# Dummy matmuls at the start, a searched order of steps and loads, and a last tile in two halves: one change to an attention and MoE kernel

## The chip, the cores and the metric

The kernel runs on one core of one Trainium2 chip. The metric is device time in microseconds (us). Each kernel was run several times, and each run tells its time, its span on the core and the mean clock that TensorE was granted. A run that is more than 1.5% above the fastest of the same kernel is called slow.

Names used below: PE is TensorE (PEld its weight loads), DVE is VectorE, ACT is ScalarE, POOL is GpSimd, SP is the queue of SyncE, which issues DMAs here. L917 is line 917 of a kernel's file, so the same statement has another number in each kernel.

## The reference, cut to what matters

```python
def _attn_ref(q, k, v):                       # 8 batches, 8 heads, 576 tokens, 64 wide
    scores = np.matmul(q, k.transpose(0, 1, 3, 2)) / np.sqrt(D)
    mask_plain = (rel >= 0) & (rel < 32)                               # heads 0-3
    mask_dil = (rel >= 0) & (rel < 128) & (rel % 4 == 0)               # heads 4-7
    ...                                       # mask, softmax
    return np.matmul(attn, v)

def _moe_ref(x, w_in, w_out):                 # x: 4608 x 512, w_in: 512 x 2048, w_out: 2048 x 512
    h = x @ w_in
    g = h * (1.0 / (1.0 + np.exp(-h)))
    return g @ w_out
```

Attention over narrow windows makes x. Two dense layers follow, and they are nearly all of the arithmetic.

## The kernel before

The kernel is written as many small steps. Kinds: `S` scores, `P` and `D` the products with v for the plain and the dilated heads, `XP` and `XD` transposes of x, `TD`, `TA`, `TB`, `TR`, `TS` transposes of q and k, `N` and `V` copies, and the steps of layer 1 (`h`, 16 blocks of w_in for each group of tokens) and layer 2 (`y`, four matmuls each). When the program is built, a small plan decides the order in which the steps are written down and, for some copies, whether DVE or ACT makes them. It keeps its own clock, on which each step and each load has an assumed cost. PE, DVE, ACT and the DMA queues get their work in the written order, and the program chooses nothing at run time.

```python
ORDER = "k0 w0a v0 r0 w1 w0b w2 w3 d1 p1 r1 o0 o1 o2 o3 v1".split()       # loads: w = w_in, o = w_out, rest q, k, v
LOAD_US = {"w": 2.57, "o": 2.57, "d": 3.2, "p": 3.4, "r": 1.7, "v": 2.5, ...}   # assumed costs
...
for t in vraws[::-1]:
    nc.vector.memset(t, 0.0)
...
    # batches 3-7: how the last steps of a batch stand in its list
    order = [("S", 0), ("S", 1), ("P", 0), ..., ("D", 1, 0), ("D", 1, 1), ("D", 1, 2), ("D", 1, 3)]
...
    # a score step, with the cost the plan assumes: 0.32 us, 0.64 us for batch 0
    st = Step(lambda ring, a=a: scores(ring, *a), 0.32 + 0.32 * (b in BIASED), ...)
...
    # x of batches 3-7 goes to DRAM and comes back transposed
    nc.sync.dma_start(out=rows, in_=oD[:, ab]...)
    yield "DMA", 3.0                          # assumed time of the store
    stored(b)
...
def group_gen(g):
    nc.sync.dma_start_transpose(out=x_of(g)[:, :, GT - n :], in_=x_s[t0 : t0 + n])
    yield "DMA", 6.0                          # assumed time of the transposed read
...
def l2(ring, tb, f4):                         # layer 2, one of four parts of an output tile
    ...
    yield "ACT", 0.50
    ob = o32.tile([P, DM], F32, tag="ob", bufs=2, name=f"ob_{g}_{tb}")
    nc.scalar.activation(ob, y, AF.Copy, scale=0.5)
    nc.scalar.dma_start(out=out[t0 + tb * P : t0 + (tb + 1) * P], in_=ob)
...
while att or l1 or l2:                        # the plan: which step is written next
    cands = [(att, it, 1.0) for it in att[:LOOK] if it[0] <= max(1, g1 - 1) + 2]
    ...
    if l1 and g1 <= g2 + 1:
        main.append((l1, l1[0], 1.3))
    cands = main + cands if side > 0.5 else cands + main
```

The softmax here doesn't subtract the row's maximum and nothing guards it: scores larger than these inputs give would overflow.

## Time and profile before

| | before |
|---|---|
| time | 316.49 us, median of three (315.64 to 317.62) |
| span of the profiled run | 314.6 us |
| PE busy | 298.2 us, 95% |
| first matmul | 5.17 us |
| first layer-1 matmul | 18.12 us, then a wait for w_in until 22.41 us |
| last matmul ends | 310.69 us |

The page of the kernel before, parts 1, 2 and 4. Part 1 has busy time, share of the span and number of instructions; part 2 has busy tenths in 40 slices of 7.9 us, with PEclk as the granted clock in tenths; part 4 is the chain of work that ended last:

```profile
PE 298.2 (95%) x2378; PEld 153.8 (49%) x2378; DVE 198.9 (63%) x498; ACT 164.9 (52%) x316; POOL 54.4 (17%) x86
PE   2979899999999999999999999999999999999995
PEclk9999999999999999999999999999999999999999
...
PE 72%; DMA 13%; DVE 7%; POOL 3%; ACT 2%; issue 1%; ACTq 0%; POOLq 0%
```

PE is the bound.

Timeline of PE, kernel before (start, duration, engine, line, operation, count, idle time before it and what ended it):

```profile
7.36 0.68 PE L614 MATMUL s<-mask_d,ident_w 128*128 128x288 f16 x2
...
16.67 0.41 PE L614 MATMUL s<-mask_d,ident_w 128*128 128x288 f16 x2
...
20.17 0.28 PE L671 MATMUL av_d<-vd,probs 128*128 128x65 f16 x4
22.41 0.61 PE L884 MATMUL h<-xA,w_in 128*128 128x256 f16 x4 [1.96 <-DMA w_in<-in_moe_w_in_dram]
...
38.69 1.02 PE L917 MATMUL y<-w_out,gT 128*128 128x512 f16 x4
```

The first two lines are the same pair of matmuls, and the later one takes 0.41 us where the earlier takes 0.68 us; the second matmul starts 0.13 us after the first there, and 0.23 us here. So PE starts at about half its later pace. PEclk does not show this, because the trace's clock records begin only at 14.57 us, with full clock; for the time before, without a record, the page prints full clock too. The next two lines show PE waiting 2 us for weights.

Two timelines of the kernel before, of the SP queue and of PE, at the point where x of a group comes back from DRAM and layer 1 uses it:

```profile
201.54 2.02 SPq L445 DMA_TRANSPOSE xR<-x_s  x1
...
210.47 1.02 PE L884 MATMUL h<-xR,w_in 128*128 128x512 f16 x4
```

The trace's semaphore records put the landing of that transfer at 206.16 us, so x lies ready 4.3 us before its first use.

The end, ACT's timeline of the kernel before:

```profile
310.73 0.60 ACT L928 ACTIVATE ob<-y 128x512 f32<-128x512 f32 x1 [2.85 <-PE y L917]
311.35 0.34 ACTq L929 DMA_DIRECT2D out_dram<-ob  x1
```

### The profile page before, as it was taken

To read this page: it belongs to the slowest core of one execution; us is meant where nothing else is said; L and a number is where in the kernel's file an instruction comes from. 1 tells how busy PE (TensorE), PEld (TensorE's weight loads), DVE (VectorE), ACT (ScalarE), POOL (GpSimd) and SP (SyncE) were. 2 spreads that over 40 slices of the span, in tenths; PEclk is the share of its full clock that TensorE was granted. 3 is DMA by queue.
4 is the path that set the end of the run, shared out by engine and by line. 5 is a ranking of instruction groups with operands and counts; after the bars stand their busy time and mean duration, and the time that the engine had idled before them with its cause. 6 is when DMAs were issued, how large, how long until landed. Compare 5 with 4: busy or idle time off the path is not lost.

```text
span 314.6 us, 6109 instructions
## 1 busy us (share of the span) xinstructions
PE 298.2 (95%) x2378; PEld 153.8 (49%) x2378; DVE 198.9 (63%) x498; ACT 164.9 (52%) x316; POOL 54.4 (17%) x86
## 2 busy tenths in 40 slices
PE   2979899999999999999999999999999999999995
PEld 1658665554545444444454445444444444444441
DVE  6479987799798677855687578548860552355000
ACT  7567774776656465445564544557443453355111
POOL 8854723001800040005000310000000000000000
PEclk9999999999999999999999999999999999999999
DMA  8999999997999969998998899941165001100221
GB/s 107 178 203 191 172 191 205 204 193 134 159 193 196 208 111 208 185 227 151 197 198 196 136 202 195 233 125 52 52 87 169 0 35 43 57 33 2 90 76 67
DMA packets 107092, 44.53 MB, mean 142 GB/s; under 512 B 73272, under 2 KB 102456, under 8 KB 107064
## 3 DMA queue, kind: packets, MB, share of 16 engines
q0 software_dynamic: 48528, 19.86, 51.9%
q1 hardware_dynamic: 53352, 14.85, 27.8%
q10 hardware_dynamic: 5184, 9.44, 8.6%
q8 instruction: 18, 0.29, 0.4%
q14 instruction: 10, 0.08, 0.1%
HBM read 39.81 MB, written 18.28 MB: 185 GB/s over the span
## 4 chain that ended last, share of the span: by engine, by line
PE 72%; DMA 13%; DVE 7%; POOL 3%; ACT 2%; issue 1%; ACTq 0%; POOLq 0%
PE y L917 35%; PE h L884 32%; DMA vp<-in_v_dram 5%; DMA w_in<-in_moe_w_in_dram 3%; DMA nat<-kq_s 3%; DVE gT L895 2%; DMA nat<-in_k_dram 2%; PE s L626 2%; PE av_d L671 2%; PE av_p L671 1%; DVE probs L644 1%; DVE oP L675 1%; POOL w_out L232 1%; DVE oD L675 1%; POOL vp L182 1%
## 5 line engine op out<-in xcount | busy, mean ns | idle before, releaser
L917 PE MATMUL y<-w_out,gT 128*128 128x512 f16 x576 | 138.1, 379 | 0.9 <-ACT ob L928 0.8
L895 DVE SCALAR_TENSOR_TENSOR gT<-th,h 128x512 f16<-128x512 f32 (+1 forms) x160 | 99.0, 629 | 56.8 <-ACT th L893 56.6
L893 ACT ACTIVATE th<-h 128x512 f32<-128x512 f32 (+1 forms) x160 | 88.9, 557 | 83.3 <-PE h L884 67.8
L884 PEld LDWEIGHTS <-w_in 128*128 128x128 f16 x640 | 59.0, 97 | 58.7 <-issue 4.7
L917 PEld LDWEIGHTS <-gT 128*128 128x128 f16 x576 | 53.9, 98 | 60.8 <-issue 1.1
L884 PE MATMUL h<-xR,w_in 128*128 128x512 f16 x320 | 77.4, 379 | 0.1
L884 PE MATMUL h<-xA,w_in 128*128 128x512 f16 (+1 forms) x320 | 63.2, 336 | 4.2 <-DMA w_in<-in_moe_w_in_dram 2.0
L928 ACT ACTIVATE ob<-y 128x512 f32<-128x512 f32 x36 | 21.5, 597 | 40.8 <-PE y L917 40.7
L635 ACT ACTIVATE probs<-s 128x768 f16<-128x768 f32 (+2 forms) x31 | 24.2, 780 | 12.3 <-PE s L626 11.9
L671 PEld LDWEIGHTS <-probs 128*128 128x128 f16 x448 | 21.7, 98 | 13.7 <-DVE probs L644 1.8
L675 DVE TENSOR_TENSOR oD<-av_d,rcps 72x256 f16<-72x256 f32 x64 | 26.9, 421 | 2.2
L675 DVE TENSOR_TENSOR oP<-av_p,rcps 96x256 f16<-96x256 f32 x48 | 20.2, 421 | 1.6
L639 ACT ACTIVATE probs<-s 128x288 f16<-128x288 f32 (+2 forms) x40 | 17.9, 472 | 1.5 <-ACT ob L928 0.9
L644 DVE TENSOR_TENSOR probs<-probs,mask_p 128x768 f16<-128x768 f16 x21 | 11.6, 554 | 10.7 <-ACT probs L635 10.3
L422 POOL COPY fence<-kqT 128x1 f16<-128x1 f16 x10 | 1.8, 190 | 93.3 <-DMA kqT<-kq_s 93.3
L671 PE MATMUL av_d<-vd,probs 128*128 128x65 f16 x256 | 14.0, 196 | 0.2 <-DVE vd L506 0.2
L644 DVE TENSOR_TENSOR probs<-probs,mask_d 128x576 f16<-128x576 f16 (+1 forms) x23 | 11.9, 518 | 3.4 <-ACT probs L639 1.6
L674 DVE RECIPROCAL rcps<-av_d 72x4 f32<-72x4 f32 x64 | 11.0, 172 | 2.7 <-PE av_d L671 2.5
L671 PE MATMUL av_p<-vp,probs 128*128 128x65 f16 x192 | 11.4, 193 | 0.7 <-DVE probs L644 0.6
L165 POOL DMA_DIRECT2D vraw<-in_v_dram x16 | 10.8, 677 | 6.2 <-DVE rcps L674 2.5
L674 DVE RECIPROCAL rcps<-av_p 96x4 f32<-96x4 f32 x48 | 8.2, 171 | 4.6 <-PE av_p L671 4.6
L178 POOL DMA_DIRECT2D vp<-in_v_dram x7 | 10.3, 1467 | 2.9 <-PE s L626 1.8
(89 smaller groups left out, 145.5 us busy)
## 6 DMA issues: line engine op xcount, KB each, us to landing
out_dram<-ob ACTq DMA_DIRECT2D x36, 256.0 KB, 2.1
kq_s<-in_k_dram POOLq DMA_DIRECT2D x5, 576.0 KB, 10.3
kq_s<-in_q_dram POOLq DMA_DIRECT2D x5, 576.0 KB, 12.9
vp<-in_v_dram POOLq DMA_DIRECT2D x7, 384.0 KB, 7.9
w_out<-in_moe_w_out_dram POOLq DMA_DIRECT2D x4, 512.0 KB, 11.0
vraw<-in_v_dram POOLq DMA_DIRECT2D x8, 224.0 KB, 5.3
w_in<-in_moe_w_in_dram POOLq DMA_DIRECT2D x3, 512.0 KB, 11.0
x_s<-oP SPq DMA_DIRECT2D x10, 144.0 KB, 1.9
```

Of the source, the lines that this page charges most:

```text
L165: nc.gpsimd.dma_start(out=vraw[p0 : p0 + m1 - m0, ab].rearrange("p h r d -> p h (r d)"), in_=src[m0:m1],)
L635: nc.scalar.activation(p2, both[:, :, :n], AF.Exp, scale=scale)
L639: nc.scalar.activation(p2[:, i], sp[i][:, :n], AF.Exp, scale=scale)
L644: nc.vector.tensor_tensor(p2, p2, mk, ALU.mult)
L671: nc.tensor.matmul(a[:, i, : D + 1], lhs(i), rhs(i), start=True, stop=True)
L674: nc.vector.reciprocal(rcp[:n], a[:n, :, D : D + 1])
L675: nc.vector.tensor_tensor(o, a[:n, :, :D], rcp[:n, :, None].broadcast_to([n, HN, D]), ALU.mult)
L884: nc.tensor.matmul(h[:, :w], w_in16[:, c, f * P : (f + 1) * P], x_g[:, c], start=(c == 0), stop=(c == HP - 1),)
L893: nc.scalar.activation(th[:, :w], h[:, :w], AF.Tanh, scale=0.5)
L895: nc.vector.scalar_tensor_tensor(gTs[g][:, f, :w], th[:, :w], 1.0, h[:, :w], ALU.add, ALU.mult)
L917: nc.tensor.matmul(y, gTs[g][:, f, tb * P : (tb + 1) * P], w_out16[:, f], start=(f == 0), stop=(f == NFF - 1),)
L928: nc.scalar.activation(ob, y, AF.Copy, scale=0.5)
```

## The change

The intent: raise PE's clock in time that is idle anyhow, fill the holes between matmuls with an order that an offline search found, and shorten the end.

```diff
-    ORDER = "k0 w0a v0 r0 w1 w0b w2 w3 d1 p1 r1 o0 o1 o2 o3 v1".split()
-    LOAD_US = {"w": 2.57, "o": 2.57, "d": 3.2, "p": 3.4, "r": 1.7, "v": 2.5, ...}
+    ORDER = "k0 r0 w0b v0 w0a w1 w2 w3 d1 p1 o0 r1 o1 o2 o3 v1".split()
+    LOAD_US = {"w": 2.57, "o": 2.57, "d": 3.2, "p": 3.0, "r": 2.3, "v": 2.57, ...}
...
-    for t in vraws[::-1]:
-        nc.vector.memset(t, 0.0)
+    warm = vraws[1].rearrange("p a h r d -> p (a h r d)")
+    nc.vector.memset(warm[:, :GT], 0.0)
+    y_warm = ps_y.tile([P, GT], F32, tag="y", name="y_warm")
+    for n in range(8):
+        nc.tensor.matmul(y_warm, warm[:, :P], warm[:, :GT], start=True, stop=True)
+    nc.vector.memset(warm[:, GT:], 0.0)
+    nc.vector.memset(vraws[0], 0.0)
...    (the three step lists in another order; of batches 3-7:)
-                ("S", 0), ("S", 1), ("P", 0), ("P", 1), ("V", 0), ("S", 2), ("S", 3), ("P", 2),
-                ... ("D", 0, 1), ("D", 0, 2), ("D", 0, 3), ("D", 1, 0), ("D", 1, 1), ("D", 1, 2),
-                ("D", 1, 3),
+                ("S", 2), ("S", 0), ("P", 1), ("S", 3), ("S", 4), ("S", 1), ("S", 5), ("P", 0),
+                ... ("D", 1, 1), ("D", 1, 3), ("D", 0, 1), ("D", 0, 2), ("D", 1, 2), ("D", 1, 0),
+                ("D", 0, 0),
...    (x is stored when a counter says that its parts are done, since their order is now free)
...    (the costs that the plan assumes:)
-                    lambda ring, a=a: scores(ring, *a), 0.32 + 0.32 * (b in BIASED), ...
+                    lambda ring, a=a: scores(ring, *a), 0.17 + 0.32 * (b in BIASED), ...
-                lambda ring, f=f: l1(ring, f), 0.01 + w / 595, ...
+                lambda ring, f=f: l1(ring, f), w / 593, ...
...    (layer 2: 0.8633 for 0.87; the last output tile in two halves, the second half's copy:)
+            half = (c1 - c0) // 2
+            nc.scalar.activation(ob[:, :half], y[:, :half], AF.Copy, scale=0.5)
+            nc.scalar.dma_start(out=rows[:, c0 : c0 + half], in_=ob[:, :half])
+            nc.vector.tensor_scalar(ob[:, half:], y[:, half:], 0.5, None, ALU.mult)
+            nc.sync.dma_start(out=rows[:, c0 + half : c1], in_=ob[:, half:])
...    (the limits by which the plan picks)
-        cands = [(att, it, 1.0) for it in att[:LOOK] ...]
+        cands = [(att, it, LIM_PAIR if it[1].mate else LIM_ATT) for it in att[:LOOK] ...]   # 0.4, 1.1
-            main.append((l1, l1[0], 1.3))
+            main.append((l1, l1[0], LIM_L1))                                             # 1.8
-        cands = main + cands if side > 0.5 else cands + main
+        cands = main + cands if side > SIDE else cands + main                            # 0.9
+        if pick is None and g2 < SPARE and l2[0][1].rings and ...:                       # SPARE = 6
+            l2[0][1].rings = ["y", "x", "z"]
```

So there are six parts: dummies, loads, lists, costs, limits and tail. The costs are four numbers (a score step, a layer-1 step, a layer-2 step, the copy of an output tile).

## The prediction

> **What bounds the kernel now.** TensorE. The summary has PE busy 298.2 of 314.6 us (95%), the chain of waits is 72% PE, and from 234 us on it is nothing but layer-1 and layer-2 matmuls back to back (four 512-column matmuls in 0.86 us) until 310.7 us. The two layers alone come to about 248 us at that pace; attention's small matmuls add some 30 us (estimate, from start-to-start times in the timeline). So roughly 36 us is start, tail and holes; only that can be won: 5.2 us before the first matmul; about 6 us of holes and slow matmuls up to 30 us; about 9 us in 30-80 us; about 9 us in 80-240 us (much of it attached to the score matmuls, "issue" before their weight loads, which the change does not remove); 4 us tail.
>
> **Step by step.**
>
> 1. *Dummy matmuls.* [...] a pair of 288-column bias matmuls takes 0.68 us at 7.4 us and 0.41 us at 16.7 us, although the windows view prints a granted clock of 1.00 there. Eight cold 512-column matmuls are about 3.4 us, in idle time, so free. They could shorten batch 0's attention by 2 to 3 us. But group 0's layer 1 needs all of w_in, whose last block stays at its place (it lands near 27.5 us, estimated from the releases of the queue's waits). Its four feature blocks then need 1.7 us, so group 0 ends at 29.3 us at best; now near 29.8. Gain 0.5 us, up to 2 if attention runs ahead better.
>
> 2. *Load order.* w0b now lands before w1, so the 2.0 us wait of PE for w_in (at 20.4-22.4 us) shrinks or moves to 22-27 us: the same bytes must come first. o0 before r1 lets the first layer-2 step start some 2 us before its present 38.7 us; PE waits 0.9 us for DVE near there.
>
> 3. *New order and thresholds.* 32-44 us is DVE-bound (3.8 of 4 us busy per window), 44-49 us waits for vp (lands 49.2 us), 60-76 us is DVE-bound again. Batch 1's dilated averages now come before its plain ones, so DVE works while vp is awaited; SPARE lets layer 2 take the x and z buffers when nothing else is ready. I expect 3 us of the 9 in 30-80 us, 1.5 us of the 9 in 80-240 us.
>
> 4. *Last tile in halves.* After the last matmul now: 0.60 us copy on ACT, then the DMA. Two quarter copies on ACT and DVE at once, smaller DMAs: 0.3 to 0.5 us.
>
> **Sum.** 0.7 + 3 + 1.5 + 0.4, about 5.5 us: 311.0 us, range 307.5 to 314.5. Nearly all of it is on the critical path, since PE is; off it is most of the warm-up.
>
> **What would show it.** 288-column bias matmuls 0.12 us apart before 10 us; first layer-1 matmul near 19.8 us instead of 18.1, and a new wait for w_in after it; group 0's layer 1 still ending at 29-30 us; first layer 2 near 36-37 us; PE denser in 44-52 us; final stretch of pure matmuls unchanged but earlier; last copy under 0.3 us.
>
> **What would make it wrong.** Warm-up too short, or followed by too long a gap, to raise the clock; warm attention running far ahead and gaining over 2 us; transfers landing later than the order assumes, so that PE, strictly in order, stands behind a missing operand; thresholds that fill the later holes much better (below 308).

The 2 to 3 us for batch 0's attention are an estimate of mine. The sum 0.7 + 3 + 1.5 + 0.4 is 5.6 us, written as about 5.5. What step 1 calls eight cold matmuls took 3.59 us in the trace of the changed kernel, starting up to 0.43 us apart, where matmuls of 512 columns start 0.22 us apart later on. Of the two risks named for the clock, that trace shows the second: full clock ended at 8.99 us, in a wait of PE of 1.97 us. That a warm-up can be too short was a guess of mine.

## The result, and the profile after

The changed kernel took 312.63 us in the median of six runs (311.31 to 316.78), against 316.68 us for the kernel before. The ratio of the fast runs is 0.9853 (95% interval 0.9816 to 0.989). A ratio here is the mean time of one kernel's fast runs over that of the other's fast runs of the same rounds, so it is not quite the ratio of the quoted medians. The time lies within the predicted range, 1.6 us above the point.

The median hides something: two of the six runs were slow, at 316.1 and 316.8 us. All twelve runs of the changed kernel (six more came with the experiments) with their mean granted clock:

| mode | us (mean clock) |
|---|---|
| seven runs, mean 312.1 us | 311.31 (1.0), 311.61 (0.988), 311.64 (1.0), 312.10 (1.0), 312.39 (1.0), 312.66 (0.999), 312.88 (1.0) |
| five runs, mean 316.3 us | 315.31 (0.982), 316.02 (0.994), 316.11 (0.984), 316.78 (0.984), 317.38 (0.984) |

The split at 315 us is mine. By the 1.5% rule three of the five longer runs are slow; 315.31 and 316.02 us count as fast in their set and in its ratio. The kernel before is not quite free of slow runs either: two of its 51 runs in all sets were slow (322.96 and 1724 us).

Parts 1, 2 and 4 of the page of the changed kernel, whose profile is of a fast run with a span of 309.8 us:

```profile
PE 299.4 (97%) x2402; PEld 155.5 (50%) x2402; DVE 195.8 (63%) x498; ACT 164.7 (53%) x318; POOL 54.5 (18%) x86
PE   6789989999999999999999999999999999999995
PEclk9599999999999999999999999999999999999999
...
PE 85%; DVE 5%; DMA 5%; ACT 3%; issue 1%; POOL 1%; ACTq 0%; DVEq 0%; POOLq 0%
```

The 5 in PEclk says that the second slice (7.7 to 15.5 us) ran at little over half clock. The records of the trace are finer: full clock from 5.58 us for 3.413 us, half clock from 8.99 to 15.82 us, then full. All records of this trace last 3.413 us or a multiple of it, but for the last, which the end of the trace cuts; one such length is called a window below. In this trace full clock came early, at 5.58 us after the dummies where the first record of the kernel before is at 14.57 us, but for a single window. The timeline of PE, changed kernel:

```profile
1.19 3.59 PE L192 MATMUL y_warm<-vraw 128*128 128x512 f16 x8 [1.19 <-DVE vraw L189]
...
6.81 0.41 PE L620 MATMUL s<-mask_d,ident_w 128*128 128x288 f16 x2
...
9.71 0.85 PE L582 MATMUL ta_q<-ident_w,nat 96*64 96x96 f16 x16 [1.97 <-DMA nat<-in_q_dram]
...
11.13 0.66 PE L620 MATMUL s<-mask_d,ident_w 128*128 128x288 f16 x2
...
22.40 1.91 PE L892 MATMUL h<-xA,w_in 128*128 128x256 f16 x16
24.14 0.42 PE L733 MATMUL xd<-ident_w,oD 72*128 72x72 f16 x8
24.40 7.16 PE L892 MATMUL h<-xA,w_in 128*128 128x256 f16 x64
...
37.30 1.03 PE L925 MATMUL y<-w_out,gT 128*128 128x512 f16 x4
```

The 288-column pair is fast at 6.8 us (0.41, starts 0.13 us apart) and slow again at 11.1 us (0.66, starts 0.21 us apart). Between them PE stood 1.97 us for q. The wait for w_in is gone, and layer 1 starts at 22.40 us and runs without a stop.

Where the gain comes from is read best by counting work. I gave each real matmul its start-to-start time at full clock (0.216 us for 512 columns, 0.109 for 256, 0.029 for 65, and so on; dummies count zero) and summed those that had started by a given time. The sums are mine, from the trace's start times:

| time, us | 20 | 30 | 50 | 80 | 140 | 180 | 240 |
|---|---|---|---|---|---|---|---|
| work started, before | 7.6 | 14.8 | 30.5 | 57.6 | 114.8 | 152.7 | 211.1 |
| work started, after | 6.4 | 15.0 | 32.1 | 60.0 | 118.7 | 157.1 | 215.2 |
| after is ahead by | -1.2 | 0.2 | 1.7 | 2.4 | 3.9 | 4.5 | 4.1 |

(The differences were taken before rounding.) So at 30 us the whole change is 0.2 us ahead. That is not the dummies' gain: by the same count the kernel without them (no_dummies, below) is about 0.4 us ahead there. Between 30 and 80 us come 2.2 us, between 80 and 240 us 1.7 us. From the start of the last matmul to the end it is 4.3 us before (310.31 to 314.6) and 3.6 us after (306.18 to 309.8).

The end, ACT's and DVE's timelines of the changed kernel:

```profile
306.49 0.28 ACT L943 ACTIVATE ob<-y 128x128 f32<-128x128 f32 x1 [1.36 <-PE y L925]
306.80 0.34 ACTq L944 DMA_DIRECT2D out_dram<-ob  x1
...
306.80 0.29 DVE L945 TENSOR_SCALAR ob<-y 128x128 f32<-128x128 f32 x1 [20.61 <-ACT ob L943]
```

The two quarter copies do not run at once. DVE starts when ACT is done ("<-ACT ob L943"), and together they take the 0.60 us that one copy took. What is won at the end comes after them: from the issue of the last DMA to the end of the span it is 3.25 us before (311.35 to 314.6) and 2.7 us after (307.12 to 309.8); the last DMA now carries a quarter of the bytes, and it goes out by SP's queue instead of ACT's; no run separates the two.

This gain does not come in every run. From the start of the last matmul to the end, the four traced kernels with a whole last tile need 4.30 to 4.32 us. Of the ten with halves, six need 3.65 or 3.66 us, but old_loads needs 3.81, slack_x_cold 4.33, kept_warm_own 4.53 and no_dummies 4.68. In no_dummies PE's last matmul ended at 308.72 us, and ACT's last copy still stood until 309.55 us for an earlier store of an output tile, since there are two buffers for such tiles. ACT's timeline of no_dummies:

```profile
309.55 0.28 ACT L940 ACTIVATE ob<-y 128x128 f32<-128x128 f32 x1 [2.15 <-DMA out_dram<-ob]
```

The lines that answer to those of x at its group start, SP queue and PE of the changed kernel:

```profile
208.15 1.98 SPq L450 DMA_TRANSPOSE xR<-x_s  x1
...
211.34 1.04 PE L925 MATMUL y<-w_out,gT 128*128 128x512 f16 x4
212.32 1.02 PE L892 MATMUL h<-xR,w_in 128*128 128x512 f16 x4
```

x landed at 212.28 us (semaphore records) and was used at 212.32. The margin of 4.3 us is gone. Over the four groups that start while attention still runs:

| margin from landing of x to first use, us | group 5 | group 6 | group 7 | group 8 |
|---|---|---|---|---|
| before | 3.0 | 2.8 | 4.3 | 4.6 |
| after | 0.7 | 0.0 | 0.0 | 0.6 |

A margin of 0.0 (0.04 in the trace) means that the matmul started as soon as x landed. In this fast run it cost little: PE stood 0.19 us at group 6, and no idle time shows at group 7. The stores of x share the SP queue with the transposed reads. In this trace it was held 1.31 to 1.80 us by one transposed read of kqT, 1.35 to 2.13 us by one of x and 2.39 to 3.64 us by one of nat, where the timeline shows them alone. One of nat held it from 192.90 to 196.48 us, and the store of x that comes next on it followed at 196.58.

### The profile page after: what moved, and what is told of

It is laid out like the page before. It is cut to its first block, busy times and chain, and to the rows that moved or that the text cites. A ratio compares the mean times of both kernels' runs of the same rounds, so it can differ in the third digit from the quotient of the medians.

```text
span 309.8 us, 6177 instructions
## 1 busy us (share of the span) xinstructions
PE 299.4 (97%) x2402; PEld 155.5 (50%) x2402; DVE 195.8 (63%) x498; ACT 164.7 (53%) x318; POOL 54.5 (18%) x86
## 4 chain that ended last, share of the span: by engine, by line
PE 85%; DVE 5%; DMA 5%; ACT 3%; issue 1%; POOL 1%; ACTq 0%; DVEq 0%; POOLq 0%
PE y L925 38%; PE h L892 36%; PE s L632 3%; PE av_d L677 3%; DMA nat<-in_q_dram 2%; PE av_p L677 2%; DMA xR<-x_s 1%; DVE probs L650 1%; DMA x_s<-oD 1%; DVE gT L903 1%; PE s L620 1%; ACT probs L641 1%; ACT ob L938 1%; ACT kqD L510 1%; DVE oP L681 1%
## 5 line engine op out<-in xcount | busy, mean ns | idle before, releaser
L925 PE MATMUL y<-w_out,gT 128*128 128x512 f16 (+1 forms) x592 | 137.8, 373 | 0.0
L925 PEld LDWEIGHTS <-gT 128*128 128x128 f16 x592 | 55.1, 98 | 57.5
L892 PE MATMUL h<-xA,w_in 128*128 128x512 f16 (+1 forms) x320 | 62.1, 336 | 0.0
L938 ACT ACTIVATE ob<-y 128x512 f32<-128x512 f32 (+1 forms) x36 | 21.3, 591 | 42.6 <-PE y L925 42.6
L681 DVE TENSOR_TENSOR oD<-av_d,rcps 72x256 f16<-72x256 f32 x64 | 26.9, 420 | 2.2
L681 DVE TENSOR_TENSOR oP<-av_p,rcps 96x256 f16<-96x256 f32 x48 | 20.2, 421 | 1.6
L645 ACT ACTIVATE probs<-s 128x384 f16<-128x384 f32 (+2 forms) x38 | 17.2, 477 | 1.1 <-PE s L632 1.1
L677 PE MATMUL av_d<-vd,probs 128*128 128x65 f16 x256 | 15.4, 196 | 1.2 <-DVE oD L681 0.6
```

Source lines behind the costliest of these rows:

```text
L645: nc.scalar.activation(p2[:, i], sp[i][:, :n], AF.Exp, scale=scale)
L677: nc.tensor.matmul(a[:, i, : D + 1], lhs(i), rhs(i), start=True, stop=True)
L681: nc.vector.tensor_tensor(o, a[:n, :, :D], rcp[:n, :, None].broadcast_to([n, HN, D]), ALU.mult)
L892: nc.tensor.matmul(h[:, :w], w_in16[:, c, f * P : (f + 1) * P], x_g[:, c], start=(c == 0), stop=(c == HP - 1),)
L925: nc.tensor.matmul(y, gTs[g][:, f, tb * P : (tb + 1) * P], w_out16[:, f, c0:c1], start=(f == 0), stop=(f == NFF - 1),)
```

## The experiments

Theory A: the dummies are worth almost nothing, because what PE waits for until about 50 us is data. Rival B: they are worth the 2 to 3 us that half a clock costs by my estimate in the prediction. A second question is which of the other five parts carries the gain, and a third what makes the slow runs. All kernels gave correct results.

### Dummies: the changed kernel again, without them, and they alone

The first run is the changed kernel as it is.

> The changed kernel once more, on the same chip as its variants. Ratio to before again 0.985 (0.981 to 0.989). Two of the first six runs were slow (316 us, mean clock 0.984); [...] about a third of these runs is slow again.

Measured: 313.98 us median (six runs, in the table above), ratio 0.99 (0.9845 to 0.9956). Three of these six are in the slow mode.

The second is the changed kernel without the dummies:

```diff
-    y_warm = ps_y.tile([P, GT], F32, tag="y", name="y_warm")
-    for n in range(8):
-        nc.tensor.matmul(y_warm, warm[:, :P], warm[:, :GT], start=True, stop=True)
```

> The changed kernel without the 8 dummy matmuls, all else kept. Theory A (the first trace: clock raised at 5.6 us for one window, then halved from 9.0 to 15.8 us, work done by 30 us only 0.2 us ahead of before): the dummies are worth 0 to 0.5 us, so 312 to 313 us, and the slow runs of 316 us vanish if the dummies cause them. Rival B (the dummies are worth the 2 to 3 us that half a clock costs): 314.5 to 315.5 us.

Measured: 312.77 us median (311.34 to 314.91), ratio 0.9869 (0.9829 to 0.9909). Rival B fails, and Theory A holds within the noise: without the dummies the kernel is about as fast as with them. The mean of its six runs is 312.9 us, that of the twelve with dummies 313.8 us, and that of their seven shorter runs 312.1 us. No run is above 315, where five of twelve are with dummies.

The third is the kernel before with the dummies:

```diff
-    for t in vraws[::-1]:
-        nc.vector.memset(t, 0.0)
+    warm = vraws[1].rearrange("p a h r d -> p (a h r d)")
+    nc.vector.memset(warm[:, :GT], 0.0)
+    y_warm = ps_y.tile([P, GT], F32, tag="y", name="y_warm")
+    for n in range(8):
+        nc.tensor.matmul(y_warm, warm[:, :P], warm[:, :GT], start=True, stop=True)
+    nc.vector.memset(warm[:, GT:], 0.0)
+    nc.vector.memset(vraws[0], 0.0)
```

> The kernel before with the 8 dummy matmuls alone. Theory A: within 0.7 us of before (ratio 0.998 to 1.001), since the last block of w_in lands at 27.5 us whatever PE does. Rival B: 2 to 3 us faster (0.991 to 0.994).

Measured: 315.72 us (314.82 to 316.95), ratio 0.9959 (0.9926 to 0.9993). That is a little better than Theory A allowed and less than Rival B's 2 to 3 us, though the interval reaches the edges of both (0.998 and 0.994). Its trace holds the best argument for A: there the clock rose at 5.50 us, fell at 12.33 and stayed at half until 22.57 us, so that its work was 1.5 us behind the kernel before at 30 us. At 50 us the two were level. What was lost at PE early was given back in a stretch in which PE of the kernel before stands anyhow, for w_in (2.0 us until 22.41) and then for DVE and ACT (1.1 and 0.5 us between 28 and 52 us). I cannot say what the 1.3 us of this kernel are.

### Keeping the clock up, first try: a miss

11 dummies instead of 8, and 24 more before the first plain transposes, in the hole at 7.6 to 9.7 us.

```diff
-    for n in range(8):
+    for n in range(11):
...
+            if (hp, nm) == (1, "q"):
+                fill = tps.rearrange("p r m -> p (r m)").bitcast(F32)
+                for _ in range(24):
+                    nc.tensor.matmul(fill, warm[:, :P], warm[:, : fill.shape[1]], start=True, stop=True)
```

> The changed kernel with 11 dummies instead of 8 and 24 more (192 columns) in the hole before the plain transposes of batch 0 (7.6 to 9.7 us), so that the clock does not fall back. Theory A with the bound by w_in (last block lands near 26.8 us, 1.7 us of layer 1 after it): clock 1.00 from about 5 us on, first layer-1 matmul at 19.2 to 20.5 us, group 0's layer 1 ends 28.5 to 29 us instead of 31.4 with 16 of the 80 matmuls of group 1, total 0.5 to 1.2 us below the changed kernel. Rival B: 2 to 3 us below. Rival C (clock falls back all the same): same or up to 1 us slower.

Measured: 340.05 us. The reason is an error of mine, and the timeline of PE of this kernel shows it:

```profile
7.28 0.54 PE L636 MATMUL s<-kqD 64*128 64x72 f16 x8
35.93 3.71 PE L583 MATMUL ta_q<-vraw 128*128 128x192 f16 x24 [28.11 <-DMA vraw<-in_v_dram]
```

`warm` is a view of a buffer into which a load of batch 1 goes. That load is written down earlier in the program than the new matmuls, so they waited 28 us for it. The run says nothing of the theories, but it shows what a filler matmul must not read.

### Keeping the clock up, mended

```diff
+                fill = tps.rearrange("p r m -> p (r m)").bitcast(F32)[:, : W + P]
+                for _ in range(28):
+                    nc.tensor.matmul(fill, ident, ident_w, start=True, stop=True)
```

> Mend of kept_warm, whose 24 extra matmuls read a buffer that a load of batch 1 writes at 36 us, so that PE stood until then. Now 11 dummies, and 28 of 160 columns on the identity, which nothing writes later. Theory A (arrival of w_in, w_out and vp bounds 20 to 50 us): clock 1.00 from about 5 us on without a fall, first layer-1 matmul near 19.2 to 20.5 us, but work done by 50 us within 0.7 us of the changed kernel's, total 311.3 to 312.5 us and no run above 314. Rival B (a warm start is worth 2 to 3 us): 309 to 310 us. Rival C: the clock falls back all the same; then times spread as with 8 dummies.

Measured: 315.58 us (312.57 to 318.35), ratio 0.9952 (0.9902 to 1.0003). The profiled run was a slow one, which was luck. In it the clock rose at 5.16 us and stayed up, as intended, until 216.79 us. Layer 1 began at 21.9 us, later than I expected, and by 30 us the work started was 15.4 us against 15.0 in the changed kernel. At 40 us the two were level (24.0), and at 50 us this kernel was 1.1 us behind (31.0 against 32.1), because PE waited for v ("PE av_p L681 <- DMA vp<-in_v_dram: 1.1, 1, 1.1" among its waits). So in this trace a start at full clock gained nothing that lasts, which is against Rival B and more than Theory A had claimed. Five of the six runs were at 315.0 us or above, so "no run above 314" failed, and the profile tells why for one of them. The timeline of PE and two windows of the same trace (for each engine busy time and count, then PEclk, DMA share and GB/s):

```profile
212.86 1.04 PE L929 MATMUL y<-w_out,gT 128*128 128x512 f16 x4
216.51 1.63 PE L896 MATMUL h<-xR,w_in 128*128 128x512 f16 x4 [2.62 <-DMA xR<-x_s]
217.93 0.43 PE L681 MATMUL av_p<-vp,probs 128*128 128x65 f16 x4
218.17 1.90 PE L896 MATMUL h<-xR,w_in 128*128 128x512 f16 x4
```

```profile
213.00:217.00 4.00, 1.38 (x6) 0.48 (x5) 0.56 (x1) 1.42 (x3) 0.00 (x0) 0.97 0.46 130
217.00:220.00 3.00, 3.00 (x12) 1.27 (x11) 1.57 (x4) 0.60 (x1) 0.00 (x0) 0.50 0.01 3
```

PE stood 2.62 us for x at the place where the changed kernel has a margin of 0.0. Then the clock was at half for one window (216.79 to 220.20 us), and two sets of four layer-1 matmuls took 1.63 and 1.90 us instead of 1.02 and 1.03. A full window at half clock costs half of 3.41 us, 1.7 us. The wait and the window together are 4.3 us, close to the 4.2 us between the two modes of the changed kernel. (This run itself is 5.8 us longer than the shortest of its kernel, and its end took 0.9 us more, as said above.)

The profile of no_dummies shows the same place in a milder form (PE's timeline):

```profile
211.97 1.04 PE L922 MATMUL y<-w_out,gT 128*128 128x512 f16 x4
214.58 1.02 PE L889 MATMUL h<-xR,w_in 128*128 128x512 f16 x4 [1.57 <-DMA xR<-x_s]
```

That run took 314.91 us, the longest of its six; the clock did not fall (PEclk 1.00 from 160 to 240 us), and the longer end (4.68 us for 3.65) is another 1.0 us of it.

### Undoing one part: lists, loads, limits

```diff
 old_lists:       the three step lists of before, all else as changed
 old_loads:       ORDER and LOAD_US of before, all else as changed
 old_thresholds:  LIM_ATT 1.0, LIM_PAIR 1.0, LIM_L1 1.3, SIDE 0.5, SPARE 0, all else as changed
```

> The changed kernel with the three step lists of before; dummies, loads, thresholds and tail kept. If the lists carry most of the gain: 315 to 317 us. If thresholds and loads do: 312 to 313.5 us. My guess 314.5 us.

Measured: 324.33 us (323.93 to 325.41), ratio 1.0249 (1.0203 to 1.0295).

> The changed kernel with the load order and load times of before. Theory: o0 before r1 lets layer 2 start 1.4 us earlier, and that is kept, so 313 to 314 us, the first layer-2 step back at 38.5 us or later. Rival: the loads do not matter, 312 to 312.7 us.

Measured: 321.86 us (319.12 to 325.72), ratio 1.0137 (1.0075 to 1.0199).

> The changed kernel with the picking limits of before (1.0, 1.0, 1.3, 0.5, and no spare buffers for layer 2). Theory: the 1.7 us gained between 80 and 180 us are theirs, so 313.5 to 314.5 us, with the loss in that stretch. Rival: it is the lists alone, then within 0.5 us of the changed kernel.

Measured: 312.71 us (312.09 to 314.75), ratio 0.9888 (0.9839 to 0.9937).

The limits are worth nothing in time that these runs can show; my expectation that they carry 1.7 us failed. The other two are worse than the kernel before with everything undone (old_loads by 1.4%; its interval lies above 1). The lists do not cost 8 us and the loads 5 us in any sense that could be added up: the lists, the loads and the numbers of the plan came as one set, and a part of it put back alone meets a plan with which it may not fit. In old_lists PE waits for DVE (waits of PE: us in total, times, longest us):

```profile
PE h L893 <- DVE gT L904: 4.0, 8, 0.8
PE y L926 <- DVE gT L904: 1.8, 4, 0.8
```

In old_loads the profiled run waits for x (the same view). It was a slow one of 325.72 us, so it does not tell why the three fast runs took 319.1 to 322.7 us:

```profile
PE h L892 <- DMA xR<-x_s: 5.3, 2, 5.0
PE h L892 <- DVE gT L903: 3.4, 6, 1.2
```

The wait of 5.0 us stands at the same group as that of kept_warm_own, and here too the clock was at half for the window at its end (220.55 to 223.97 us).

### More margin for x: a rival and a failed cure

Theory X: the slow mode is PE standing at the first layer-1 matmul of a group. Theory C: it is the early fall of the clock after the dummies. The edit makes the plan reckon with a slower return of x, and so write more work ahead of that matmul.

```diff
-                yield "DMA", 3.0      # store of x, both places
+                yield "DMA", 4.0
-        yield "DMA", 6.0              # transposed read of x
+        yield "DMA", 8.0
```

> The changed kernel with three numbers of its plan altered: a store of x is reckoned at 4 us instead of 3, its transposed read at 8 instead of 6. That puts at least 12.2 us of PE work (counted in the order, at the pace of the trace) between the last product of a batch and the first layer-1 matmul that needs it, instead of 10.2 to 10.9. Theory X: the runs of 315 to 317 us come from PE standing at that matmul (margin 0.0 to 0.7 us in the first trace, 2.8 to 4.6 before; 2.6 us wait plus one window at half clock in the slow profile). Then no run above 314, all within 311 to 313, no wait of layer 1 for xR over 0.3 us. Theory C (the runs of 315 to 317 come from the early fall of the clock after the dummies): two or three of six runs are above 315 again.

Measured: 318.52 us (317.24 to 319.80), ratio 1.0076 (1.0043 to 1.0109).

> The same without the 8 dummies. Theory X with dummies worth nothing: the same as slack_x within 0.6 us, 311.3 to 312.5 us, no run above 314. Rival: 1 us or more above slack_x.

Measured: 318.43 us (315.83 to 320.56), ratio 1.0061 (1.001 to 1.0112).

Both are slightly slower than the kernel before (0.8% and 0.6%, the intervals above 1) and some 6 us slower than the changed kernel's shorter runs, so the cure failed. The wait for x is indeed gone (margins 0.4, 4.1, 0.3 and 2.9 us in slack_x). The hole has moved to another transfer that had no margin either. PE's timeline of slack_x:

```profile
150.70 0.35 PE L632 MATMUL s<-nat 64*128 64x96 f16 x8
152.99 0.37 PE L632 MATMUL s<-kqT 64*128 64x72 f16 x12 [1.95 <-DMA kqT<-kq_s]
153.30 1.15 PE L925 MATMUL y<-w_out,gT 128*128 128x512 f16 x4
154.24 3.50 PE L892 MATMUL h<-xR,w_in 128*128 128x512 f16 x8
```

PE stands 1.95 us for the transposed keys of the next batch, and again the clock is at half for the window that follows (154.09 to 157.50 us): eight layer-1 matmuls take 3.50 us instead of 1.89. The profile of slack_x_cold has the same wait (2.10 us) and a fall at 153.86 us, without any dummies. The fall is not what makes these kernels slow: two runs of slack_x whose mean clock was 1.0 took 317.24 and 317.49 us.

These two traces show what a mean clock can tell. One window of 3.41 us at half clock lowers the mean over a span of some 310 us by 0.0055. slack_x_cold, with the late window alone, has 0.995. slack_x, with two half-clock windows after the dummies (7.31 to 14.14 us) and the late one, has 0.984. The fast run of the changed kernel with 0.988 has the two early windows alone. So four of the five longer runs of the changed kernel (0.982 to 0.984) fit three half-clock windows, and the fifth (0.994) fits one. The mean does not tell where the windows lay: only_dummies has 0.982 with three early windows and no late one, and a run of old_thresholds has 0.984 at 312.36 us. Theory C therefore does not explain the longer runs: early windows at half clock went with short runs there, and in the run of 0.988, which took 311.61 us. Nor does a mean of 1.0 say that the clock was up from the start: the records of after_again's profile (mean 1.0) begin at 13.35 us, those of the kernel before (mean 1.0) at 14.57 us.

A late wait, followed by a half-clock window in four of the five traces that show one, is the best candidate. It is seen where layer 1 needs x of group 7 in kept_warm_own (2.62 us), old_loads (5.02 us) and, without the fall, no_dummies (1.57 us), and at another transfer in slack_x and slack_x_cold. For a slow run of the changed kernel itself it is not shown, since its profiles fell in fast runs. Two rivals were not tried apart. One is the early rise and fall of the clock as something that makes late waits more frequent. The other is the new limits: with the old ones the margins of groups 5 to 8 are 0.1, 3.1, 0.4 and 1.8 us (old_thresholds) and 0.1, 2.3, 0.4 and 1.3 us (lists_loads_costs, below), more than in the changed kernel at three of the four groups, and none of these ten runs is above 315 us.

### Building up instead: lists and loads, then costs

The kernel before with the new lists and loads (and the counters for the stores of x), and then the same with the new costs.

```diff
 lists_loads_costs against lists_loads:
-                    lambda ring, a=a: scores(ring, *a), 0.32 + 0.32 * (b in BIASED), ...
+                    lambda ring, a=a: scores(ring, *a), 0.17 + 0.32 * (b in BIASED), ...
-                lambda ring, f=f: l1(ring, f), 0.01 + w / 595, ...
+                lambda ring, f=f: l1(ring, f), w / 593, ...
-                    lambda ring, tb=tb, f4=f4: l2(ring, tb, f4), 0.87, [],
+                    lambda ring, tb=tb, f4=f4: l2(ring, tb, f4), 0.8633, [],
-            yield "ACT", 0.50
+            yield "ACT", 0.08 + DM / 1200
```

> The kernel before with the new step lists and the new load order alone (and the counters that let the stores of x follow any order): old limits, no dummies, whole last tile. If lists and loads together carry the gain: 312.5 to 314 us. If they need the new limits and costs: 316 us or more.

Measured: 316.81 us (315.22 to 319.08), ratio 1.0022 (0.9986 to 1.0057). So lists and loads by themselves give nothing at the end. Yet at 80 us the work started was ahead of before by 2.4 us, exactly as in the changed kernel. It was lost afterwards: at 160 us the lead was 1.0 us, where the changed kernel has 4.0.

> lists_loads (316.8 us) with one thing more: the costs by which the plan reckons a score step (0.17 us for 0.32), a layer-1 step, a layer-2 step and its copy, as the changed kernel has them. Still no dummies, old limits, whole last tile. Its order on PE is then that of old_thresholds but for the dummies and the halves of the last tile. Theory K (the truer costs carry what the lists and loads alone did not give: they decide where the plan puts everything after 80 us): 312.8 to 313.8 us, ratio to before 0.988 to 0.992. Rival (the missing 3 to 4 us are the dummies, the limits or the tail): 316 us or more.

Measured: 313.30 us (312.95 to 314.27), ratio 0.9907 (0.9887 to 0.9928). Theory K holds for the size. Four assumed costs are worth 3.5 us between these two kernels (316.81 and 313.30), on top of the new lists and loads. They leave the arithmetic and the 2378 matmuls as they are; what changes is the order that the plan writes and also its choice between DVE and ACT for some copies (of the 18 copies of xA of 192 columns ACT makes 9 instead of 12), and no run separates order and choice. The two were not timed in the same rounds, but on the same chip, where the kernel before had medians of 316.35 and 316.62 us. (One run of before in the second set took 1724 us; it is not a fast run and is left out of the ratio.) At 160 us the lead is 2.6 us. The last tile is still whole, there are no dummies, the limits are old, and the six runs lie within 1.3 us of each other. On PE this kernel's order is that of old_thresholds, but for the dummies and the split of the last tile; that one has 312.71 us, so dummies and split together are worth some 0.6 us between these medians, which come from two chips. The end alone is 0.67 us shorter in its trace (3.65 us for 4.32).

Which of the four matters is not shown, since single costs were not tried apart. By an estimate the score step moves the plan's clock most. A pair of score steps occupies PE for 0.43 to 0.48 us in the chain of waits of the kernel before ("PE s L626 x20"), so 0.22 to 0.24 us each, against 0.32 assumed. With 51 such steps and 0.15 us taken off each, the plan's clock runs 7.7 us less ahead by the end. The new 0.17 is not the measured cost either: it lies about as far below it as the old one above. So it is shown that these four numbers work together with the lists and loads, and not that truer numbers do.

## Why the prediction was right or wrong

The time lay in the range (307.5 to 314.5). The sum was 5.6 us; the profiled runs differ by 4.8 us. That it came so near is in part luck: of its four terms the first (0.7 us) is not seen, the second was 0.8 us too large, and the last two came about in another way than predicted. Point by point:

1. *Dummies: little of it reaches the end.* Right that it is little: 0.5 to 0.7 us predicted; the whole change is 0.2 us ahead at 30 us, and no_dummies is as fast within the noise. The reason was only half right. I took the last block of w_in for the limit and the clock for raised. In the trace the clock was up for one window only (5.58 to 8.99 us) and fell during a wait of 1.97 us for q. w_in was no limit: layer 1 began at 22.40 us instead of the predicted 19.8 and met no wait. Group 0's layer 1 ended near 29.6 us (24.40 us plus twelve blocks of 0.436 us), in the predicted 29 to 30. I had named "too long a gap" as a risk, and the clock did fall in this wait.
2. *The wait for w_in shrinks or moves.* Wrong in form: it vanished, because the attention steps written before layer 1 finished only at 22.4 us. *Layer 2 near 36 to 37 us*: 37.30.
3. *3 us in 30-80, 1.5 us in 80-240.* Measured 2.2 and 1.7 us. The stretches were right; the second was credited to the wrong part. The prediction put it down to the new order and the thresholds, SPARE among them. With the old thresholds the kernel is as fast (312.71 us), and the new lists and loads with the old costs lose their lead again after 80 us. The costs, which the prediction does not mention at all, carry it on top of lists and loads: without them these end at 316.81 us, with them at 313.30. That is the step that failed.
4. *Two quarter copies at once.* Wrong in mechanism, right in size (0.3 to 0.5 us predicted, 0.7 us measured from the last matmul's start). The copies run one after the other and save nothing; 0.55 us is saved after the last issue and 0.1 us by the narrower last matmul. In four of the ten traces with halves the gain is smaller or gone.
5. *What would make it wrong.* "PE, strictly in order, stands behind a missing operand" was listed as a risk to the time. It is the likely reason why five of twelve runs are 4.2 us longer, seen in sibling kernels and not in those runs. I had not looked for it where it probably lay: the trace of before showed 2.8 to 4.6 us of margin for x, of which the new order leaves 0.0 to 0.7.

No kernel here beats both in a way that is clear of noise. Leaving the dummies out of the changed kernel gives 312.9 us in the mean of all runs against 313.8 us with them, but the seven shorter runs with them have 312.1 us. Which is better is not shown.

## What to carry to other kernels

Where an order is planned at build time, the assumed costs are part of the kernel and have to be tried with it: here four numbers were worth 3.5 us, and new lists and loads without them gave nothing at the end. Look at the spread and at how long each operand lies ready before its use, not only at the median: here the margin of x fell from 2.8 to 4.6 us to 0.0 to 0.7 us, and the runs fell into two modes. Before warming up PE, ask whether PE is what the next microseconds wait for, and whether a wait follows: here the clock fell back in a 2 us wait for q, and the one trace in which it stayed up (kept_warm_own) was no further than the changed kernel by 50 us.
